# Second layer of the last two units as seven block products of 96 tokens

## The chip, the cores and the metric

The kernel runs on one core of a Trainium2 chip. The metric is device time in microseconds (us) of one execution. Engines are called as in the profile: PE is TensorE (PEld its weight loads), DVE is VectorE, ACT is ScalarE, POOL is GpSimd, and SP issues the DMAs.

## What is computed

Attention with a pooled and a banded part gives `x` (4 batches of 576 tokens, 512 features). Then come a Fourier mixing of `x`, a normalisation, a two-layer network and a gated convolution layer:

```python
u = x + real(fft(fft(x, axis=1), axis=2))
un = (u - mean(u)) / sqrt(var(u) + 1e-6)
x = u + maximum(un @ w_ch1, 0) @ w_ch2          # 512 -> 2048 -> 512
gate = sigmoid(sum over k of conv_w[k] * x shifted by 4 - k tokens)
out = (gate * (x @ w_val)) @ w_out
```

The change concerns the product with `w_ch2` (the second layer).

## The kernel before

**Units.** The two-layer network and the gated layer run over 12 units of 192 tokens, numbered 0 to 11, three to a batch. Features lie on the partitions. Each float32 operand is split into two float16 numbers, high and low, and each product of two operands is three matmuls (`PASS`: high by high, high by low, low by high), each with its own weight load.

**First layer.** In units 6 to 11 (`SEVEN`) the first layer is done by `seven(i)`, i from 0 to 3: weights and activations are cut into two by two blocks, tokens into two halves of 96, and seven block products with sums of blocks take the place of eight. The tile `r1` collects the results (DVE adds, one ACT copy); its four rows are the blocks of h: r[0:2] the first half of the hidden features, r[2:4] the second, each for 2 by 96 tokens in two chunks. `relu` turns them into `hh` and `hl` (high on ACT, low on DVE). The sums of weights that these products need are made once on DVE (`sums_w1`), stored in DRAM as `sums` and loaded for each unit (`load_sums`): into a place among the weights for even i, and from unit `S_TWO` on into tiles `sm` in the pool qkv for odd i.

**Second layer.** `c_group(g)`, g from 0 to 7, multiplies two chunks of 128 hidden features with w_ch2: 2 chunks by 4 output blocks by 3 passes, 24 matmuls of 192 tokens. The eight groups of a unit make 192 matmuls, accumulated in two PSUM banks `pc` (pool ps_c). `fin` adds the banks to X with two DVE instructions.

**Gated layer.** `split_y` splits the new X into `yy` (high on ACT, low on DVE), `conv` and for unit 11 `conv_last` make the taps of the convolution (DVE; one block of unit 11 on PE, `tps`), `val` multiplies with w_val, the gated product is split into `gh` and `gl`, and `out_tile` multiplies with w_out, 12 matmuls of 512 columns to a tile of 128 tokens. Units 10 and 11 share three such tiles.

**Order.** A table `ORDER` fixes, engine by engine, the order of all instructions of the whole kernel after the load of the constants, SP's DMAs among them. Nothing is chosen at run time: an engine, and SP's queue too, waits at an instruction whose input is late, and all that stands behind it waits with it. `SLOT` says which buffer of a pool a tile takes.

Of the kernel before, what the change touches and what calls it, by code (L numbers as in the profile page):

```python
# [21 lines left out]
UT = 192  # L22
# [47 lines left out]
450.0 430.1 430.0 499.0 488.1 488.0 467 499.1 488.2 491.1 491.0 492.1 491.2 492.0 492.2 499.2-3 493.1 493.0 493.2  # L70
546.0-1 539 535 546.2-3 545.0 550.1 550.0 545.1 553 554 559.1 559.0 609 639
# [6 lines left out]
170.1-2 210 186 187 172.0 197.1 197.0 247.0 171.0 211 171.1-2 172.3 172.1 172.4 212 193.1 172.5 172.2 174.0-1 227  # L78
247.1-2 193.2 247.3 174.2 197.2-3 228 197.4 224.0-1 253.0 197.5 173 247.4 229 258 247.5-6 188 259 253.1 239.0 239.3
232 189 239.4 239.1 255.2 230 239.5 239.2 255.0-1 255.3 265 224.2-3 225 234 233 241 249.3 249.0 253.2 269 224.5 224.4  # L80
253.3-5 292.0 236 292.1 274 257.0 257.3 253.6-7 292.2 249.1 249.4 278 243 249.5 249.2 253.8-10 302.0 246 253.11 292.3
257.1-2 261.0 253.12 302.2 253.13 261.1 257.4-5 263.3 263.0 299.0 302.1 253.14 293.0 284 407.0 302.3 251 292.4-5 288
263.1-2 263.4 261.2 303.3 303.1 261.3 263.5 303.2 267.1 304.1 293.1 293.3 304.2-3 300 293.4 303.0 261.5 261.4 293.2
267.0 299.1 305 293.5 295 271.0 310 273.0 271.2 271.1 273.2 273.1 261.6 271.3 314 275.1 299.2 273.3 275.0 323 306.1
296.0 277.1 277.0 275.2 277.2 327 299.3-4 335 296.1 280.0 306.2 280.1 282.0 407.1 296.2 407.2 296.3-4 283.0 304.0
296.5 282.1 283.1 306.3 297.0-1 306.0 309 407.4 285 297.3-5 286 291.0-1 338 291.2 342 297.2 291.3 294.0 291.4 322
326.1 326.0 294.1-2 350.1 313.0 326.2 291.5 339 291.6 326.3 313.1 333.1 333.0 298.0 311.0 354 350.0 298.2 298.1 357
311.1 364 407.3 328.3 328.1 328.0 328.2 329.1-2 329.0 331.2 331.1 329.3 332 334.2 334.1 371 331.3 331.0 334.0 334.3
341.0 319 341.1 379 347.0 324 344 347.1-2 345.0-1 355.0 333.2 356.0 333.3 347.3-4 388 355.2 359.0 462.1 366 355.1
347.5-6 356.2 359.2 347.7 345.2 355.3 356.1 345.3 356.3 347.8 395 376.0 376.3 347.9 400 359.3 359.1 378.0-2 347.10  # L90
361.1 378.3 361.0 406.1 361.3 406.0 378.4 376.1-2 376.4 361.2 413 381.0 372.0 376.5 372.1 410 377.0 387.0 381.3 377.1
# [393 lines left out]
def attn_moe_kernel(ctx, tc, q_t, k_t, v_p, v_w, w1, w2, w_val, conv_t, w_out, c_feat, c_seq, c_band, c_eye, c_plm, out):  # L485
# [44 lines left out]
    def load(**kw):  # L530
        nc.sync.dma_start(**kw)
# [1591 lines left out]
```

## Time and profile before

| | us |
|---|---|
| median of 3 runs | 657.6 |
| lowest and highest run | 655.76 and 657.8 |
| the profiled execution | 656.75 |
| its span, first to last instruction | 654.7 |
| PE busy, share of the span | 644.5, 98% |
| DVE busy | 527.3, 81% |
| ACT busy | 355.3, 54% |
| POOL busy | 103.5, 16% |

A time of the profile is counted from the start of the span; the execution's own time is some 2 us longer than the span. "Idle before" is the time that an engine stood still before an instruction, with what ended it. Matmuls are pipelined: the time from one start to the next is what a matmul costs in a stream, not its own length.

### The profile page before, as it was taken

To read this page: it belongs to the slowest core of one execution; us is meant where nothing else is said; L and a number is where in the kernel's file an instruction comes from. 1 tells how busy PE (TensorE), PEld (TensorE's weight loads), DVE (VectorE), ACT (ScalarE), POOL (GpSimd) and SP (SyncE) were. 2 spreads that over 40 slices of the span, in tenths; PEclk is the share of its full clock that TensorE was granted. 3 is DMA by queue.
4 is the path that set the end of the run, shared out by engine and by line. 5 is a ranking of instruction groups with operands and counts; after the bars stand their busy time and mean duration, and the time that the engine had idled before them with its cause. 6 is when DMAs were issued, how large, how long until landed. Compare 5 with 4: busy or idle time off the path is not lost.

```text
span 654.7 us, 20391 instructions
## 1 busy us (share of the span) xinstructions
PE 644.5 (98%) x8626; PEld 574.5 (88%) x8627; DVE 527.3 (81%) x1138; ACT 355.3 (54%) x1057; POOL 103.5 (16%) x162
## 2 busy tenths in 40 slices
PE   9989999999999999999999999999999999999997
PEld 4668899999998887998988888997899989998995
DVE  3999989989988876789999969996778787587554
ACT  2787659788644656677444778644232332414223
POOL 0000121310121703510310153032010100100000
PEclk9959999999999999999999999999999999999999
DMA  9994583023343012332482363352524234343201
GB/s 313 393 339 165 210 309 117 20 85 138 108 126 129 2 37 69 102 115 90 137 288 82 116 215 117 112 177 77 180 85 163 98 112 133 113 146 130 99 3 48
DMA packets 44301, 89.96 MB, mean 137 GB/s; under 512 B 3391, under 2 KB 24895, under 8 KB 43186
## 3 DMA queue, kind: packets, MB, share of 16 engines
q1 hardware_dynamic: 44210, 88.67, 39.8%
q8 instruction: 67, 1.10, 0.7%
q14 instruction: 24, 0.20, 0.1%
HBM read 73.77 MB, written 16.65 MB: 138 GB/s over the span
## 4 chain that ended last, share of the span: by engine, by line
PE 85%; DVE 7%; DMA 3%; ACT 2%; POOL 1%; issue 1%; SPq 0%; ACTq 0%; DVEq 0%; POOLq 0%
PE pc L1389 25%; PE ph L1319 11%; PE ph L1340 8%; PE out L1510 7%; PE val L1494 6%; PE p L1340 6%; DVE W L522 3%; PE ab L1070 2%; PE pc L1294 1%; PE po L1761 1%; PE dO L879 1%; PE po L1604 1%; DMA raw<-in_moe_w_ch_dram 1%; PE st L1154 1%; PE sc L957 1%; PE po L1002 1%
## 5 line engine op out<-in xcount | busy, mean ns | idle before, releaser
L1389 PE MATMUL pc<-hh,W 128*128 128x192 f16 x1232 | 169.8, 246 | 0.0
L1389 PEld LDWEIGHTS <-W 128*128 128x128 f16 x1848 | 152.7, 98 | 4.0 <-issue 1.6
L1389 PE MATMUL pc<-hl,W 128*128 128x192 f16 x616 | 129.3, 246 | 0.0
L1319 PE MATMUL ph<-u,W 128*128 128x192 f16 x960 | 94.5, 246 | 0.6 <-ACT u L1199 0.6
L1319 PEld LDWEIGHTS <-W 128*128 128x128 f16 x960 | 80.2, 98 | 2.8 <-issue 1.4
L1340 PEld LDWEIGHTS <-W 128*128 128x128 f16 x1632 | 79.0, 98 | 2.7 <-issue 0.8
L522 DVE SCALAR_TENSOR_TENSOR W<-X,cw,W 128x192 f32<-128x192 f32 x160 | 62.5, 426 | 9.1 <-ACT W L1457 8.8
L1340 PE MATMUL ph<-u,W 128*128 128x96 f16 x960 | 65.1, 206 | 0.2
L1352 ACT ACTIVATE hh<-r 128x384 f16<-128x384 f32 x48 | 24.3, 519 | 71.9 <-DVE r L528 60.2
L1494 PE MATMUL val<-yy,W 128*128 128x192 f16 x576 | 59.1, 246 | 0.1
L1494 PEld LDWEIGHTS <-W 128*128 128x128 f16 x576 | 47.6, 98 | 2.0 <-issue 0.9
L1340 PE MATMUL p<-u,W 128*128 128x96 f16 x672 | 47.9, 206 | 0.0
L1510 PE MATMUL out<-W,gh 128*128 128x512 f16 x144 | 45.8, 379 | 0.0
L528 DVE TENSOR_TENSOR r<-ph,r 128x384 f32<-128x384 f32 (+1 forms) x48 | 21.8, 454 | 21.0 <-PE ph L1340 19.2
L843 ACT ACTIVATE dP<-dS,dmx 128x64 f32<-128x64 f32 x120 | 36.5, 331 | 0.4
L522 DVE SCALAR_TENSOR_TENSOR hl<-r,hh 128x384 f16<-128x384 f32 x48 | 26.2, 564 | 9.4 <-ACT hh L1352 8.9
L528 DVE TENSOR_TENSOR r<-p,r 128x192 f32<-128x192 f32 (+1 forms) x72 | 28.2, 419 | 5.5 <-PE p L1340 3.1
L1323 ACT ACTIVATE hh<-ph 128x384 f16<-128x384 f32 x40 | 19.4, 490 | 19.5 <-PE ph L1319 17.6
L522 DVE SCALAR_TENSOR_TENSOR W<-W,W 128x1024 int32<-128x1024 int32 x24 | 28.9, 1220 | 0.2
L1510 PE MATMUL out<-W,gl 128*128 128x512 f16 x72 | 27.3, 379 | 0.0
L843 ACT ACTIVATION_READ_ACCUMULATOR dP<-dS,dmx 128x1 f32 x120 | 26.9, 224 | 0.0
L1510 PEld LDWEIGHTS <-gh 128*128 128x128 f16 x144 | 14.1, 98 | 13.6
(308 smaller groups left out, 1429.5 us busy)
## 6 DMA issues: line engine op xcount, KB each, us to landing
W<-sums SPq DMA_DIRECT2D x32, 512.0 KB, 4.4
W<-in_moe_w_ch_dram SPq DMA_DIRECT2D x12, 1024.0 KB, 6.9
sm<-sums SPq DMA_DIRECT2D x16, 512.0 KB, 6.7
out_dram<-osb SPq DMA_DIRECT2D x17, 256.0 KB, 4.1
vw<-in_vw_dram SPq DMA_DIRECT2D x8, 512.0 KB, 4.8
w1f<-W SPq DMA_DIRECT2D x8, 512.0 KB, 3.1
sums<-so SPq DMA_DIRECT2D x16, 256.0 KB, 2.9
v<-in_vp_dram SPq DMA_DIRECT2D x24, 144.0 KB
```

Source lines behind the costliest of these rows:

```text
L522: return eng.scalar_tensor_tensor(out=out, in0=in0, scalar=scalar, in1=in1, op0=op0, op1=op1)
L528: return eng.tensor_tensor(out=out, in0=a, in1=b, op=ALU.add)
L843: A.activation(out=s_[:, z, a], in_=pss[par][:, z, a], func=AF.Exp, scale=SCALE, bias=mx[:, par, z, a:a + 1], accum_out=su[:, par, z, a:a ...
L879: T.matmul(out=pos[x][par * 64:par * 64 + 64, a2, o:o + nq], lhsT=vw[g][row, 2 * z + hf, c:c + D], rhs=pts[z][row, par, a2, hf * 64:hf * 6 ...
L1070: T.matmul(out=ps[0:n, c0:c1], lhsT=d[x][:, c, sd, e, n0:n0 + n], rhs=feat[:, w, c, c0:c1], start=(t == 0), stop=(t == 5),)
L1319: T.matmul(out=ps[:, e], lhsT=w1_ap(pw, kc, 2 * g + e), rhs=uh[px][:, kc, :], start=(t == 0), stop=(t == 11))
L1323: A.activation(out=h_, in_=ps, func=AF.Relu)
L1340: T.matmul(out=out[:, e * HT:e * HT + HT], lhsT=w(pw, kc, e), rhs=b_[x](px, kc), start=(kc, pw, px) == (0, 0, 0), stop=(kc, pw, px) == (1, ...
L1352: A.activation(out=h[0], in_=x, func=AF.Relu)
L1389: T.matmul(out=ps[m // 2][:, m % 2], lhsT=w2_ap(pw, kk, m), rhs=x[px][:, e], start=(kk == 0 and (pw, px) == (0, 0) and m % 2 == 0), stop=( ...
L1494: T.matmul(out=ps[:, e], lhsT=wv_ap(pw, kc, 2 * mh + e), rhs=m_["y"][px][:, kc, :], start=(t == 0), stop=(t == 11))
L1510: T.matmul(out=ps, lhsT=(gh, gl)[px][:, kc, t * 128:(t + 1) * 128], rhs=wo_ap(pw, kc), start=(n == 0), stop=(n == 11))
```

## The change

In units 10 and 11 (`BOTH`) the second layer is cut in the same way as the first. `c_seven(i)` makes seven products, each of 2 output blocks by 2 chunks by 3 passes, 12 matmuls of 96 tokens: 84 for an i, 336 for a unit in place of 192 matmuls of 192 tokens. They are accumulated in three PSUM banks, 14 areas; the third bank is taken from the pool ps_t, so the third tile of `seven` moves from there to ps_h. Three things are added for it:

- Sums of blocks of h. `seven` now writes relu back to `r1` on ACT, POOL makes four sums of 192 columns (`r2`), and these are split into `hs` (high on ACT, low on DVE, 768 columns). `hh`/`hl` of the first half are made for one of the two token halves alone.
- Sums of blocks of w_ch2. The eight float32 weight tiles are stored to DRAM (`store_w2`, 8 DMAs of 512 KB) before they are split; later `sums_w2` loads them (16 DMAs of 256 KB), scales them on ACT, makes four differences of 256 columns on POOL, splits them (high on ACT, low on POOL, 1024 columns), and stores `sums2` (16 DMAs of 256 KB), eight times over. `load_sums2` loads them for units 10 and 11 (24 DMAs, 4 MB a unit).
- `fin_seven` in place of `fin`: one ACT, eight DVE and four POOL instructions.

`S_TWO` goes from 8 to 9: unit 8 loads all its sums of w_ch1 into the one place among the weights. The tables ORDER and SLOT are new from about the middle of the kernel on; before it, only the eight stores are put into SP's order.

```diff
-S_TWO = 8
+S_TWO = 9
+BOTH = (10, 11,)
+S_F32B, S_SUMSB = 0.4, (8.0, 9.4)
...
+    def store_w2(i):
+        nc.sync.dma_start(out=w2f[i * P:(i + 1) * P, :], in_=W[AT[8 + i] + 1])
+
+    def sums_w2(i, e):
...
+        A.activation(out=x, in_=x, func=AF.Copy, scale=sc["s2"][:, 0:1])
+        for o, p, q in ((0, 1, 0), (1, 3, 1), (3, 3, 0), (2, 2, 3)):
+            G.tensor_tensor(out=x[:, o], in0=x[:, p], in1=x[:, q], op=ALU.subtract)
+        y = [mainp["S"].tile([P, 4, 256], F16, tag="S", name="to") for _ in range(2)]
+        A.activation(out=y[0], in_=x, func=AF.Copy)
+        G.tensor_tensor(out=y[1], in0=x, in1=y[0], op=ALU.subtract)
...
-            x = pst("p5", [P, 2, UT])
+            x = ps_x["t"].tile([P, 2, UT], F32, tag="t", name="p5", slot=0) if two else pst("p5", [P, 2, UT])
...
-            relu(hy, r[:, 2:4])
-            p = pst("p5", [P, UT])
+            if two:
+                A.activation(out=r[:, 2:4], in_=r[:, 2:4], func=AF.Relu)
+                A.activation(out=hy[0], in_=r[:, 2:4], func=AF.Copy)
+                V.tensor_tensor(out=hy[1], in0=r[:, 2:4], in1=hy[0], op=ALU.subtract)
+            else:
+                relu(hy, r[:, 2:4])
+            p = ps_h.tile([P, UT], F32, tag="h", name="ph") if two else pst("p5", [P, UT])
...
+            A.activation(out=r[:, 0:2], in_=r[:, 0:2], func=AF.Relu)
+            A.activation(out=hx[0][:, 0], in_=z[0], func=AF.Copy)
+            V.tensor_tensor(out=hx[1][:, 0], in0=z[0], in1=hx[0][:, 0], op=ALU.subtract)
+            y = accp.tile([P, 4, UT], F32, tag="acc", name="r2", slot=1)
+            add(G, y[:, 0], z[1], z[3])
+            for o, p, q in ((y[:, 1], y[:, 0], z[0]), (y[:, 2], z[0], z[1]), (y[:, 3], z[2], y[:, 1])):
+                G.tensor_tensor(out=o, in0=p, in1=q, op=ALU.subtract)
...
+            A.activation(out=w[:, 0], in_=y, func=AF.Copy)
+            V.tensor_tensor(out=w[:, 1], in0=y, in1=w[:, 0], op=ALU.subtract)
...
+            todo = [(1, blk(0, 0), lambda px: hx[px][:, 0]), (2, blk(1, 0), lambda px: hy[px][:, 0]),
+                    (4, sm2(2), lambda px: hy[px][:, 1]), (6, sm2(3), ws(1)), (3, blk(1, 1), ws(3)),
+                    (7, sm2(1), ws(2)), (5, sm2(0), ws(0))]
+            if i == 3:
+                todo = [todo[k] for k in (0, 3, 4, 5, 6, 1, 2)]
...
+            A.activation(out=t[:, 0], in_=ps[1], func=AF.Copy, scale=iv)
+            add(G, x11, x11, t[:, 0])
+            more(t[:, 1], ps[6], t[:, 0])
+            more(t[:, 2], ps[5], t[:, 1])
+            more(t[:, 1], ps[7], t[:, 1])
+            add(G, x12_, x12_, t[:, 2])
+            add(G, x21, x21, t[:, 1])
+            add(G, x22, x22, t[:, 1])
+            for m in range(2):
+                more(x12_[:, m], c["ps"][3][m], x12_[:, m])
+            more(x22, ps[5], x22)
+            more(x11, ps[2], x11)
+            more(x21, ps[4], x21)
...
+    for i in range(8):
+        put(S_F32B, lambda i=i: store_w2(i))
+    spread([(1.0, lambda i=i, e=e: sums_w2(i, e)) for i in range(4) for e in range(2)], *S_SUMSB)
```

Three places of the new order. First DVE at the end of unit 11, from its last `r1` to the split of X; `pc` are the PSUM banks of the second layer, `t` is the tile of `fin_seven`. Before:

```order
L528 TENSOR_TENSOR r_10959<-p_11017,r_10959 128x384
L522 SCALAR_TENSOR_TENSOR hl<-r_10959,hh 128x384 x2
L522 SCALAR_TENSOR_TENSOR gl<-W_123,gh 128x2x192
L522 SCALAR_TENSOR_TENSOR X<-pc_10571,iv_1484,X 128x2x192
L522 SCALAR_TENSOR_TENSOR X<-pc_10572,iv_1484,X 128x2x192
L522 SCALAR_TENSOR_TENSOR tap<-X,cw,tap 128x192 x4
L522 SCALAR_TENSOR_TENSOR yy<-X,s_y_9697,yy 128x768
```

Now, from the split of the sums of h on:

```order
L1451 TENSOR_TENSOR hs<-r_11506,hs 128x768
L1432 TENSOR_TENSOR hl<-r_11401,hh 128x384
L542 SCALAR_TENSOR_TENSOR W_123<-W_123,val 128x384
L542 SCALAR_TENSOR_TENSOR gl<-W_123,gh 128x2x192 x2
L542 SCALAR_TENSOR_TENSOR t_11682<-pc_11083,iv_1494,t_11682 128x192
L542 SCALAR_TENSOR_TENSOR t_11682<-pc_11084,iv_1494,t_11682 128x192 x2
L542 SCALAR_TENSOR_TENSOR X<-pc_11085,iv_1494,X 128x2x96
L542 SCALAR_TENSOR_TENSOR X<-pc_11083,iv_1494,X 128x96
L542 SCALAR_TENSOR_TENSOR X<-pc_11084,iv_1494,X 128x96
L542 SCALAR_TENSOR_TENSOR X<-pc_11084,iv_1494,X 128x2x96
L542 SCALAR_TENSOR_TENSOR X<-pc_11085,iv_1494,X 128x2x96
L542 SCALAR_TENSOR_TENSOR tap<-X,cw,tap 128x192 x2
```

Two instructions that read PSUM stood between the last matmul of the second layer and the taps; now there are eight, and two taps instead of four stand ahead of the split `yy`.

The second place is PE right behind, from the last of 12 `out` matmuls of another tile to the product with w_val. Before:

```order
L1510 LDWEIGHTS gh
L1510 MATMUL out<-W_122,gh 128x512
L1467 MATMUL tps<-X,W_123 128x192 x5
L1494 LDWEIGHTS W_121
L1494 MATMUL val<-yy,W_121 128x192
```

Now:

```order
L1648 MATMUL out<-W_122,gh 128x512
L1605 MATMUL tps<-X,W_123 128x192 x2
L1632 LDWEIGHTS W_121
L1632 MATMUL val<-yy,W_121 128x192
L1632 LDWEIGHTS W_121
L1632 MATMUL val<-yy,W_121 128x192
L1605 MATMUL tps<-X,W_123 128x192 x2
```

The five taps that PE makes are spread out: two, then two matmuls of `val`, then two, and the last one later among `val`.

The third place is POOL while batch 3 is mixed; `vr`, `ptv`, `fs` and `uc` belong to attention, mixing and normalisation, `tx` and `to` to `sums_w2`. Before:

```order
L528 TENSOR_TENSOR vr<-vr,ptv 72x256
L528 TENSOR_TENSOR uc<-X 128x384
L528 TENSOR_TENSOR uc<-uc 128x192
L1044 TENSOR_TENSOR fs<-X 128x577 x2
L528 TENSOR_TENSOR sq<-sq 128x384
```

Now:

```order
L548 TENSOR_TENSOR vr<-vr,ptv 72x256
L1293 TENSOR_TENSOR tx<-tx 128x256 x6
L1064 TENSOR_TENSOR fs<-X 128x577
L548 TENSOR_TENSOR uc<-X 128x384
L1293 TENSOR_TENSOR tx<-tx 128x256
L1064 TENSOR_TENSOR fs<-X 128x577
L548 TENSOR_TENSOR uc<-uc 128x192
L548 TENSOR_TENSOR sq<-sq 128x384
L548 TENSOR_TENSOR sq<-sq 128x192
L1293 TENSOR_TENSOR tx<-tx 128x256
L1296 TENSOR_TENSOR to<-tx,to 128x1024
```

The differences of the weights stand between POOL's work for mixing and normalisation, and the long `to` behind them.

## Rows read from the trace of the kernel before

**Rows 1.** The page's first part: busy time, share of the span and instructions.

```profile
PE 644.5 (98%) x8626; PEld 574.5 (88%) x8627; DVE 527.3 (81%) x1138; ACT 355.3 (54%) x1057; POOL 103.5 (16%) x162
```

**Rows 2.** Windows: length; busy PE, PEld, DVE, ACT, POOL; granted clock; DMA share, GB/s.

```profile
455.00:635.00 180.00, 179.96 (x2779) 169.50 (x2777) 131.65 (x310) 55.63 (x112) 10.12 (x12) 1.00 0.34 115
```

**Rows 3.** Waits of PE from 50 us on, longest first in total.

```profile
PE dO L879 <- DMA vw<-in_vw_dram: 0.9, 1, 0.9
```

**Rows 4.** PE in order of time: start, length, line, operation, count.

```profile
600.88 1.14 PE L1340 MATMUL p<-u,W 128*128 128x96 f16 x23
...
641.77 4.12 PE L1494 MATMUL val<-yy,W 128*128 128x192 f16 x48
```

**Rows 5.** DVE groups by form, 300 to 655 us: busy us, mean ns, idle before.

```profile
L522 DVE SCALAR_TENSOR_TENSOR W<-X,cw,W 128x192 f32<-128x192 f32 x115 | 45.0, 425 | 6.7 <-ACT W L1457 6.5
L522 DVE SCALAR_TENSOR_TENSOR hl<-r,hh 128x384 f16<-128x384 f32 x48 | 26.2, 564 | 9.4 <-ACT hh L1352 8.9
L528 DVE TENSOR_TENSOR r<-p,r 128x192 f32<-128x192 f32 x48 | 17.0, 355 | 5.5 <-PE p L1340 3.1 <-PE st L1154 0.5
...
L528 DVE TENSOR_TENSOR r<-p,r 128x384 f32<-128x384 f32 x24 | 13.2, 549 | 0.0
...
L522 DVE SCALAR_TENSOR_TENSOR X<-pc,iv,X 128x384 f32<-128x384 f32 x16 | 9.4, 606 | 6.0 <-PE pc L1389 6.0
...
L1200 DVE TENSOR_TENSOR u<-uc,u 128x768 f16<-128x768 f32 x7 | 6.7, 953 | 0.2 <-ACT u L1199 0.2
```

**Rows 6.** ACT groups by form, 300 to 655 us.

```profile
L1352 ACT ACTIVATE hh<-r 128x384 f16<-128x384 f32 x48 | 24.3, 519 | 71.9 <-DVE r L528 60.2 <-PE pc L1389 11.4
...
L1252 ACT ACTIVATE so<-sx,s_w 128x1024 f16<-128x1024 f32 x6 | 6.9, 1144 | 8.7 <-DVE sx L1250 7.5 <-DMA sums<-so 1.3
...
L1199 ACT ACTIVATE u<-uc 128x768 f16<-128x768 f32 x7 | 5.9, 842 | 9.1 <-PE ph L1340 5.7 <-DVE uc L1209 2.9 <-DVE uc L525 0.5
```

**Rows 7.** POOL groups by form, whole span.

```profile
L528 POOL TENSOR_TENSOR vr<-vr,ptv 72x256 f32<-72x256 f32 x12 | 10.4, 873 | 0.6
...
L525 POOL TENSOR_TENSOR dP<-dP,dsu 128x512 f32<-128x512 f32 x8 | 8.3, 1057 | 16.1 <-DVE dsu L847 13.7 <-ACT dmx L838 2.4
...
L528 POOL TENSOR_TENSOR uc<-uc 128x192 f32<-128x192 f32 x6 | 4.8, 794 | 0.3
...
L525 POOL TENSOR_TENSOR r<-r 128x192 f32<-128x192 f32 x4 | 2.0, 507 | 0.3
```

**Rows 8.** DVE and then POOL in order of time, 428 to 436 us.

```profile
428.26 0.82 DVE L522 SCALAR_TENSOR_TENSOR FL<-fF,s_x,FH 128x578 f16<-128x578 f32 x1
...
432.08 1.97 DVE L522 SCALAR_TENSOR_TENSOR FL<-fF,s_x,FH 128x578 f16<-128x578 f32 x1
...
431.70 3.63 POOL L1044 TENSOR_TENSOR fs<-X 128x577 f32<-128x577 f32 x2
```

**Rows 9.** All engines in order of time, around the end of unit 11's second layer.

```profile
637.68 0.25 PE L1389 MATMUL pc<-hh,W 128*128 128x192 f16 x1
...
637.97 0.62 DVE L522 SCALAR_TENSOR_TENSOR X<-pc,iv,X 128x384 f32<-128x384 f32 x1 [0.21 <-PE pc L1389]
...
638.98 0.92 ACT L1436 ACTIVATE yy<-X,s_y 128x768 f16<-128x768 f32 x1
...
639.94 1.01 DVE L522 SCALAR_TENSOR_TENSOR yy<-X,s_y,yy 128x768 f16<-128x768 f32 x1
...
645.73 0.38 PE L1510 MATMUL out<-W,gh 128*128 128x512 f16 x1
```

**Rows 10.** DMA issues by line: count, KB each, median us from issue to landing.

```profile
W<-sums SPq DMA_DIRECT2D x32, 512.0 KB, 4.4
...
w1f<-W SPq DMA_DIRECT2D x8, 512.0 KB, 3.1
```

**Rows 11.** SP and ACT in order of time, 125 to 133 us.

```profile
125.10 0.30 SPq L531 DMA_DIRECT2D v<-in_vp_dram  x1
...
132.04 1.15 ACT L689 ACTIVATE W<-W,s_w 128x1024 f16<-128x1024 f32 x1
```

More of the change, by code (lines that the diff above doesn't have):

```diff
@@ L82 @@
[L82 to L91, printed above, removed]
@@ L1328, in mlp_steps @@
         sm = {}
+        two = b * UPB + j in BOTH
         def seven(i):
@@ new lines, in seven, with acc2 @@
+            hh[i] = (hx, hy, w)
+        def acc2():
+            if "ps" not in c:
+                b0, b1 = (ps_c.tile([P, 5, HT], F32, tag=f"c{z}", name=f"pc{z}") for z in range(2))
+                b2 = ps_x["t"].tile([P, 4, HT], F32, tag="t", name="pc2", slot=1)
+                c["ps"] = {1: (b0[:, 0], b0[:, 1]), 6: (b0[:, 2], b0[:, 3]), 3: (b0[:, 4], b1[:, 4]),
+                           7: (b1[:, 0], b1[:, 1]), 5: (b1[:, 2], b1[:, 3]), 2: (b2[:, 0], b2[:, 1]), 4: (b2[:, 2], b2[:, 3])}
+                c["pair"] = {1: b0[:, 0:2], 6: b0[:, 2:4], 7: b1[:, 0:2], 5: b1[:, 2:4], 2: b2[:, 0:2], 4: b2[:, 2:4]}
+            return c["ps"]
@@ new lines, in c_seven @@
+        def c_seven(i):
+            ps = acc2()
+            hx, hy, w = hh.pop(i)
+            t_ = c.pop(("sum", i))
+            bank = lambda n, m: (m if n == 3 else {1: 0, 6: 0, 7: 1, 5: 1, 2: 2, 4: 2}[n])
+            blk = lambda dk, dm: lambda p, e, m: w2_ap(p, 8 * dk + 2 * i + e, 2 * dm + m)
+            sm2 = lambda s: lambda p, e, m: t_[s][:, e * 512 + p * 256 + m * 128:e * 512 + p * 256 + m * 128 + 128]
+            ws = lambda s: lambda px: w[:, px, s]
+            todo = [(1, blk(0, 0), lambda px: hx[px][:, 0]), (2, blk(1, 0), lambda px: hy[px][:, 0]),
[3 more added lines that the diff above has]
+                todo = [todo[k] for k in (0, 3, 4, 5, 6, 1, 2)]
+            seq_ = [(n, m, f, x, e, pw, px) for n, f, x in todo for m in range(2) for e in range(2) for pw, px in PASS]
+            b_ = [bank(n, m) for n, m, *_ in seq_]
+            for k, (n, m, f, x, e, pw, px) in enumerate(seq_):
+                T.matmul(out=ps[n][m], lhsT=f(pw, e, m), rhs=x(px)[:, e * HT:e * HT + HT],
+                         start=(i == 0 and b_[k] not in b_[:k]), stop=(i == 3 and b_[k] not in b_[k + 1:]))
@@ new lines, in fin_seven @@
+        def fin_seven():
+            X, iv, ps = st[b]["X"], sc["iv12"][:, 0:1], c["pair"]
+            o = PAD + j * UT
+            x11, x12_, x21, x22 = (X[:, 2 * z:2 * z + 2, o + n * HT:o + n * HT + HT] for n in range(2) for z in range(2))
+            t = prp.tile([P, 3, 2, HT], F32, tag="E", name="t2", bufs=3)
+            more = lambda o, p, q: stt(V, o, p, iv, q, ALU.mult, ALU.add)
+            A.activation(out=t[:, 0], in_=ps[1], func=AF.Copy, scale=iv)
[11 more added lines that the diff above has]
+            more(x21, ps[4], x21)
@@ L1403, in both, with both2 @@
                 sm[i] = [load_sums(b * UPB + j, i, q) for q in range(2)]
+            def both2(i):
+                c["sum", i] = load_sums2(i)
+            if two:
+                for i in range(4):
+                    steps.append(lambda i=i: (both(i), both2(i)))
+                    steps.append(lambda i=i: seven(i))
+                    if i:
+                        steps.append(lambda i=i: c_seven(i - 1))
+                steps.append(lambda: c_seven(3))
+                steps.append(fin_seven)
+                return steps
             done = []
```

593 lines of the change are left out of this document (324 added, 269 removed), and 4 rows, old and new, of the table ORDER.

## The prediction

> **What bounds the kernel now.** I read the page's first part, the windows, PE's waits, and then the timeline of PE. PE is busy 98% of the span [rows 1], and in the stretch in which units 8 to 11 run, 455 to 635 us, it is busy 179.96 of 180 us at full granted clock, 2.4 GHz [rows 2]. From 50 us on its longest wait is 0.9 us for one DMA [rows 3]. So what PE is given to do sets the time, and the reader should see that DVE (131.65 of 180 us), ACT (55.63) and POOL (10.12) have room in that stretch [rows 2]. The exception is the end: behind the last matmul of unit 11's second layer a chain through DVE and ACT leads to the last products, and there PE is covered only by what work is left over [rows 9].
>
> A busy PE says nothing of the price of one matmul, so I take that from starts in a stream. 23 matmuls of 96 tokens, each with its own weight load, take 1.14 us; a lone one is listed at 0.21 us, so (1.14 - 0.21)/22 = 0.042 us each; shorter and mixed streams give up to 0.0431, and I use 0.0428. 48 matmuls of 192 tokens take 4.12 us, a lone one 0.25: (4.12 - 0.25)/47 = 0.0824 us [rows 4].
>
> **What PE is saved.** Two units lose 192 matmuls of 192 tokens and get 336 of 96: 384 x 0.0824 = 31.6 us against 672 x 0.0428 = 28.8 us, so -2.9 us (-2.7 to -3.4 with 0.0431 and 0.042). The sum hangs on a small matmul costing half of a large one, though each has a weight load. The Trainium skill ("TensorE: Matmul & The Clock Gate", Back-to-back issue gap) speaks against that: it gives some 81 ns for a matmul in a real stream of loads and matmuls at 128 columns. By it, 672 x 0.081 = 54.4 us, and the change would lose some 23 us, an estimate from that page. The trace does not agree: its streams are such pairs, and 96 columns cost 0.043 us [rows 4].
>
> **What the other engines get.** All of this lies beside PE unless something is late.
>
> DVE: for each i the split of 384 columns becomes one of 192 (0.564 to 0.355), and 768 columns of `hs` (0.953) come in: +0.74 us, eight times 5.9; `fin_seven` has six instructions of 192 columns at 0.355 and two of 96 at under that where `fin` has two of 0.606, +1.5 us a unit [rows 5]. Together +9 us, hidden by DVE's 48 idle us of the stretch [rows 2].
>
> ACT: for each i two relus back into `r1` (0.519 each) and 768 columns (0.842), less for the halved copy, some +1.7 us, eight times 14; `sums_w2` sixteen times 1024 columns at 1.144, 18 us [rows 6]. 32 us more, beside 124 idle us [rows 2].
>
> POOL: 32 sums and 8 adds of 192 columns at 0.507 to 0.794, 20 to 32 us; 32 differences of 256 columns at up to 0.873, 28 us; eight splits of 1024, each twice the 1.057 of 512 columns, 17 us [rows 7]: some 65 to 77 us, most of it in the last 230 us, where POOL does little.
>
> DMA: the eight stores of w_ch2 come into SP's queue early. Three of them wait for weights that DVE has just made and stand ahead of loads of further weights that wait for the same DVE work, so those shift by the 0.4 us of an issue. The others stand behind loads for attention. The narrowest is that of the first w_ch2 tile, fourth behind a load issued at 125.10: by some 127 it is issued, and 3.1 us later, as w1f, landed [rows 10, 11]; its place is overwritten by an ACT instruction at 132.04 [rows 11]. So 0, and if it were later, all of ACT's queue behind it would move. Unit 8 loses its second place for sums. By my count of the order's matmuls between the last use of one and the first use of the next, 5.6 to 6.3 us are left for a load of 4.4 [rows 10] and two issues of 0.4: 0, with some 1 us to lose if two land together. The 24 new loads have over 13 us each between the last use of a buffer and the next.
>
> **The waits that it adds.** (1) The chain of the last i of unit 11. Behind the last first-layer matmul: two DVE adds (0.355, 0.549), a relu (0.52), four POOL sums one after the other (2.0 to 3.2), ACT's 0.84 and DVE's 0.95 [rows 5 to 7], with the hand-overs 5.4 to 6.6 us until the low half is there. PE's order has 90 matmuls of 96 and 26 of 192 to do meanwhile: 3.85 + 2.14 = 6.0 us. So 0 to 0.6 us of wait, I take 0.2. For the other seven i the order leaves 7 to 10 us.
>
> (2) The end. Let T be the start of the last second-layer matmul. Before, T is 637.68; X was complete at T + 0.9, the low half of `yy` at T + 3.3, and the first of the last 24 `out` began at 645.73, T + 8.05 [rows 9], with PE never waiting long. Now the product that `fin_seven` reads first ends 22 matmuls ahead of T, so DVE starts at T - 0.75 and needs six times 0.36 and two times 0.28: T + 2.0. Two of its last instructions also wait for three POOL adds that follow its first: T - 0.4 + 3 x (0.51 to 0.79) and then two DVE instructions, T + 1.8 to 2.7. I take X at T + 2.4. Then ACT's 0.92 and DVE's 1.01 [rows 9]: the low half at T + 4.5. PE has 12 `out` at 0.215, four taps at 0.36 and two `val` until T + 4.2, so it loses 0.3. DVE then has six of the eight taps of the first two blocks still to do (0.39 each): T + 6.9; tanh, the gated product and the high half, three instructions of some 0.55 with one tap between them, T + 9.0. The last `out` begin at T + 9.0 instead of 8.05: +1.0 us, with 0.3 to 1.7 as its bounds. I take 1.1 with what the split order of the taps may cost.
>
> (3) DVE beside POOL. A DVE instruction with its operands in SBUF takes much longer while POOL works: FL takes 0.82 alone and 1.97 under POOL's `fs` [rows 8], while adds from PSUM keep their length. POOL's new 70 us fall on a DVE that is 73% busy [rows 2]. If half of the 80 new instructions hold one of DVE's up for half their length, that is some 18 us of DVE; nearly all of it goes into DVE's 39 remaining idle us. I take 0.4 us for PE, with 0 and 4 as bounds.
>
> **Sum.** -2.9 + 0.2 + 1.1 + 0.4 = -1.2 us. The profiled execution of 656.75 would become 655.55. It lies 0.85 under the median, so for the median, 657.6, I say **656.4 us**. A change under 0.3%, some 2 us, can't be told from none.
>
> **Rivals.**
> - Faster: the end costs as little as its lower bound, the chains are covered, and the 0.9 us wait for `vw` [rows 3], whose load now stands earlier in SP's queue, goes too: -2.9 + 0.3 - 0.9 = -3.5, 654.1 us. For it: PE is full and the order gives every other chain 1 to 4 us of slack. Against it: eight instructions stand where two stood, on the one chain that PE waits for.
> - Slower: DVE, held up by POOL, falls behind in units 8 to 11. The three tiles of ps_h for each i now share two buffers, so a late add on DVE stops PE's next product at once; that decides if DVE's loss passes its 39 idle us, or if the loss comes in lumps of a 2 us `to` more than its slack of about 2 us. Eight `to` and eight chains with 0.3 to 0.5 us each that reach PE: +4 us, so -2.9 + 1.3 + 4 = +2.4, 660.0 us. For it: FL's 1.15 us of delay [rows 8]. The Trainium skill ("SBUF — State Buffer", Who interferes with whom) has the rule: a DVE instruction with two SBUF inputs and a GpSimd instruction that reads SBUF shut each other out for the whole instruction. The trace agrees: FL ends about when the first `fs` does.
> - It does not do what it says: a small matmul costs as much as a large one, +23 us, 680 us. Nothing in the rows bears it out.
>
> **How the numbers follow.** Forecast, within 0.3% of before: 0.45, its own range 655.6 to 658.5. Faster rival 0.32, slower 0.22, no saving 0.01. So faster 0.32, same 0.45, slower 0.23. The range reaches to the faster rival and to the slower one's time, 653.9 to 660.2, and leaves out those 2 in 10 that lie past either.
>
> **What would show it.** PE: 672 matmuls of L1479 at 0.043 us; if they come at 0.08 the first term is wrong. End: X complete 2.0 to 2.9 us behind the last second-layer matmul, and the last `out` 9 us behind it. PE waits naming `hs` or `hl` in the last i; waits of PE for DVE's `r` adds in units 8 to 11, and DVE instructions of 0.36 listed at 0.8 and more, would speak for the slower rival. A wait for `W<-sums` or `sm` would mean that unit 8's single place or SP's queue is too tight. The forecast is wrong if the waits of PE from 300 us to the end of unit 11 come to over 2 us, or if the end costs nothing.

## The result: 1% slower, and the profile after

| | before | after |
|---|---|---|
| median of 4 runs, us | 657.55 | 663.71 |
| lowest and highest run | 655.76 and 657.8 | 662.62 and 664.69 |
| the profiled execution, its span | 656.75, 654.7 | 664.69, 662.9 |

The ratio is 1.0098, 95% interval 1.0082 to 1.0115: 6.4 us slower by the ratio (the medians differ by 6.2), outside the range of the prediction. All line numbers below are those of the kernel spoken of; an edit that adds lines shifts them.

The first part of the page of after, against [rows 1]: PE is as busy as before, though it has less to do.

```profile
PE 644.9 (97%) x8914; PEld 573.3 (86%) x8915; DVE 547.6 (83%) x1158; ACT 383.4 (58%) x1099; POOL 174.7 (26%) x242
```

Windows of after (length; busy PE, PEld, DVE, ACT, POOL; granted clock; DMA share, GB/s). In the stretch of [rows 2] PE now stands still for 2.0 us, and DVE is 82% busy. The second and third line are the place where the granted clock fell: full until 407 us, behind two waits of PE, then 0.66 on the mean of 5 us, which is time at the lower level, 1.2 GHz. (1 - 0.66) x 5 = 1.7 us are lost there beside the waits themselves.

```profile
455.00:635.00 180.00, 178.00 (x2949) 164.42 (x2948) 146.93 (x324) 77.93 (x145) 68.30 (x82) 1.00 0.63 202
...
398.00:407.00 9.00, 7.37 (x90) 5.42 (x88) 7.86 (x19) 5.85 (x22) 5.80 (x6) 1.00 0.75 247
407.00:412.00 5.00, 5.00 (x67) 5.00 (x67) 2.52 (x11) 3.19 (x12) 0.00 (x0) 0.66 0.11 25
```

Waits of PE in after from 80 us on (total, times, longest). Before, the longest was 0.9 us for vw [rows 3]; the waits for ET, h, DS, r, dP and tm are new.

```profile
PE dO L899 <- DMA vw<-in_vw_dram: 1.6, 1, 1.6
PE po L1022 <- ACT ET L1017: 1.3, 1, 1.3
PE ph L1341 <- ACT h L1343: 1.2, 1, 1.2
PE p L1400 <- DVE DS L542: 0.8, 1, 0.8
PE ph L1400 <- DVE r L548: 0.8, 2, 0.6
PE dPT L882 <- DVE dP L545: 0.7, 1, 0.7
PE ph L1377 <- ACT u L1219: 0.6, 1, 0.6
PE pc L1479 <- DMA tm<-sums: 0.6, 1, 0.6
```

The end of unit 11 in after, all engines in order of time, against [rows 4, 9]. The 20 small matmuls take (1.01 - 0.21)/19 = 0.042 us each, as was reckoned. T is 644.79; X is complete at 646.89 (T + 2.1), the low half of `yy` at T + 4.1, and the last `out` begin at T + 8.5, where it was T + 8.05.

```profile
643.05 1.01 PE L1479 MATMUL pc<-hs,tm 128*128 128x96 f16 x20
...
644.79 0.21 PE L1479 MATMUL pc<-hh,tm 128*128 128x96 f16 x1
...
645.11 1.78 DVE L542 SCALAR_TENSOR_TENSOR X<-pc,iv,X 128x192 f32<-128x192 f32 x5
...
647.88 1.02 DVE L542 SCALAR_TENSOR_TENSOR yy<-X,s_y,yy 128x768 f16<-128x768 f32 x1 [0.16 <-ACT yy L1574]
...
653.29 0.60 PE L1648 MATMUL out<-W,gh 128*128 128x512 f16 x2
```

So the loss is neither in the new matmuls nor mainly at the end. It comes in three places: 90 to 165 us, where PE does exactly what it did before and the only new thing is the eight stores; 386 to 411 us; and the waits for DVE in units 7 to 11. Each has a theory of its own, tested below: theory 1, the stores hold up the loads behind them; theory 3, two loads stand at a bad place in SP's queue; theory 2, POOL's sums hold DVE up.

### The profile page after: what moved, and what is told of

Read it like the earlier page. It is cut to its first block, busy times and chain, and to the rows that moved or that the text cites. A ratio compares the mean times of both kernels' runs of the same rounds, so it can differ in the third digit from the quotient of the medians.

```text
span 662.9 us, 21279 instructions
## 1 busy us (share of the span) xinstructions
PE 644.9 (97%) x8914; PEld 573.3 (86%) x8915; DVE 547.6 (83%) x1158; ACT 383.4 (58%) x1099; POOL 174.7 (26%) x242
## 4 chain that ended last, share of the span: by engine, by line
PE 77%; DVE 10%; DMA 8%; POOL 2%; ACT 2%; issue 1%; SPq 0%; DVEq 0%; POOLq 0%; ACTq 0%
PE pc L1515 18%; PE ph L1377 11%; PE ph L1400 7%; PE val L1632 6%; PE out L1648 6%; PE p L1400 5%; PE pc L1479 4%; DVE W L542 4%; PE ab L1090 2%; PE pc L1352 1%; DMA tm<-sums 1%; DMA raw<-in_moe_w_ch_dram 1%; PE po L1899 1%; DMA vw<-in_vw_dram 1%; PE po L1022 1%; PE po L1742 1%
## 5 line engine op out<-in xcount | busy, mean ns | idle before, releaser
L1515 PE MATMUL pc<-hh,W 128*128 128x192 f16 x1008 | 138.4, 246 | 0.0
L1515 PEld LDWEIGHTS <-W 128*128 128x128 f16 x1512 | 125.0, 98 | 4.6 <-issue 1.8
L1515 PE MATMUL pc<-hl,W 128*128 128x192 f16 x504 | 104.5, 246 | 0.0
L1400 PEld LDWEIGHTS <-W 128*128 128x128 f16 x1728 | 84.7, 99 | 4.5 <-issue 1.5
L1377 PEld LDWEIGHTS <-W 128*128 128x128 f16 x960 | 80.2, 98 | 3.6 <-issue 2.0
L1400 PE MATMUL ph<-u,W 128*128 128x96 f16 x1056 | 69.2, 207 | 1.0 <-DVE r L548 0.8
L542 DVE SCALAR_TENSOR_TENSOR W<-X,cw,W 128x192 f32<-128x192 f32 x160 | 66.0, 453 | 2.6 <-ACT W L1595 2.3
L1400 PE MATMUL p<-u,W 128*128 128x96 f16 x672 | 51.6, 209 | 0.8 <-DVE DS L542 0.8
L1632 PEld LDWEIGHTS <-W 128*128 128x128 f16 x576 | 47.5, 98 | 2.8 <-issue 1.3
L548 DVE TENSOR_TENSOR r<-ph,r 128x192 f32<-128x192 f32 (+1 forms) x56 | 24.5, 438 | 18.7 <-PE ph L1400 17.3
L1293 POOL TENSOR_TENSOR tx<-tx 128x256 f32<-128x256 f32 x32 | 26.4, 828 | 48.1 <-ACT tx L1291 26.9
L1412 ACT ACTIVATE hh<-r 128x384 f16<-128x384 f32 x32 | 15.8, 519 | 29.5 <-DVE r L548 27.2
L542 DVE SCALAR_TENSOR_TENSOR hl<-ph,hh 128x384 f16<-128x384 f32 x40 | 21.9, 551 | 5.9 <-ACT hh L1381 5.7
```

The costliest lines, as they stand in the source:

```text
L542: return eng.scalar_tensor_tensor(out=out, in0=in0, scalar=scalar, in1=in1, op0=op0, op1=op1)
L548: return eng.tensor_tensor(out=out, in0=a, in1=b, op=ALU.add)
L1293: G.tensor_tensor(out=x[:, o], in0=x[:, p], in1=x[:, q], op=ALU.subtract)
L1377: T.matmul(out=ps[:, e], lhsT=w1_ap(pw, kc, 2 * g + e), rhs=uh[px][:, kc, :], start=(t == 0), stop=(t == 11))
L1400: T.matmul(out=out[:, e * HT:e * HT + HT], lhsT=w(pw, kc, e), rhs=b_[x](px, kc), start=(kc, pw, px) == (0, 0, 0), stop=(kc, pw, px) == (1, ...
L1412: A.activation(out=h[0], in_=x, func=AF.Relu)
```

## Experiments

Medians in us and ratios to the kernel before, which ran beside them on the same chip each time (its median 656.96 to 657.53):

| kernel | median | ratio, 95% interval |
|---|---|---|
| e1 before + stores | 661.74 | 1.0062 (1.0039 to 1.0086) |
| e2 stores on ACT's queue | 660.67 | 1.0048 (1.0030 to 1.0066) |
| e3 little work for POOL | 661.39 | 1.0059 (1.0038 to 1.0080) |
| e4 two loads moved | 662.09 | 1.0068 (1.0042 to 1.0093) |
| e5 = e2 and e4 | 657.48 | 1.0010 (0.9994 to 1.0025) |
| e6 = e5, sums moved | 658.47 | 1.0010 (0.9997 to 1.0023) |
| e7 = e6, last tiles exchanged | 658.07 | 1.0006 (0.9993 to 1.0019) |
| e8 = e7, ACT's sums further back | 660.83 | 1.0050 (1.0031 to 1.0069) |
| e9 = e5, little work for POOL | 655.98 | 0.9967 (0.9949 to 0.9986) |
| e10 = e5, sums at other places | 659.16 | 1.0022 (1.0006 to 1.0038) |
| e11 three stores behind the loads | 662.81 | 1.0080 (1.0051 to 1.0108) |
| e12 the changed kernel again | 664.69 | 1.0116 (1.0094 to 1.0138) |

Gains below are differences of ratios from the first 1.0098 of the changed kernel, where nothing else is said. Its second ratio, 1.0116 in e12, shows that a difference of 0.2% between two chips says little by itself.

**The stores: e1, e2, e11, e12.** e1 adds to the kernel before what the first half of the change adds, and no more:

```diff
+    w2f = dram.tile([8 * P, 1024], F32, tag="w2f", name="w2f")
+    def store_w2(i):
+        nc.sync.dma_start(out=w2f[i * P:(i + 1) * P, :], in_=W[AT[8 + i] + 1])
```

> The kernel before, with nothing added but the eight stores of w_ch2 (nobody reads them), at the same places of SP's queue as in the changed kernel. Theory 1 (the stores hold up the weight loads behind them, and PE with them, at 105 to 165 us): 2.0 to 2.5 us slower than before, about 659.9 us, and the same new waits of PE as in the changed kernel (about 1.2 us for h near 105 us, 0.7 us for dP near 118 us). Rival (those waits come from something else, or from chance): 657.5 us, and PE's first half as before.

Slower by 0.62%, 4.1 us, more than expected. Its two longest waits of PE, and the windows around the first: here the clock fell behind it, (1 - 0.72) x 6 = 1.7 us.

```profile
PE ph L1297 <- ACT h L1299: 2.1, 1, 2.1
PE dO L889 <- DMA vw<-in_vw_dram: 1.8, 1, 1.8
```

```profile
100.00:106.00 6.00, 4.07 (x26) 3.77 (x24) 5.50 (x8) 6.00 (x25) 0.00 (x0) 1.00 0.27 94
106.00:112.00 6.00, 5.80 (x25) 5.80 (x26) 5.16 (x7) 5.03 (x20) 0.00 (x0) 0.72 0.81 263
```

e2 has the changed kernel issue the same stores from ACT, behind the instruction that reads the tile anyway:

```diff
-        nc.sync.dma_start(out=w2f[i * P:(i + 1) * P, :], in_=W[AT[8 + i] + 1])
+        nc.scalar.dma_start(out=w2f[i * P:(i + 1) * P, :], in_=W[AT[8 + i] + 1])
```

> The changed kernel, with the eight stores issued by ACT, each right behind the sum of squares that reads the same tile, instead of by SP; the rest of SP's queue stays in its order. Theory 1: 1.5 to 2.5 us faster than the changed kernel, 661.2 to 662.2 us; the waits of 1.2 and 0.7 us near 105 and 118 us go. Rival (it is the bytes of the stores on the DMA engines, not SP's queue, or ACT's issues cost as much): 663.7 us.

It gained 0.50%, 3.3 us, and its interval lies wholly under that of the changed kernel; the waits for h and dP are gone, 0.2 us is left of them. Its wait for vw is 0.3 us where it was 1.6, so not all of the gain lies between 90 and 165 us. But e2 moves the stores in time as well as to another queue, so it doesn't tell why they hurt. The trace of after does. SP issues the two loads into `raw` (weights as they come, which DVE then converts) at 87.52, no later than before (87.75 there). Yet DVE, whose rows follow in order of time, waits 3.68 us for the first (2.34 before). The same wait is 4.62 us in e1, 4.43 in e12 and 2.70 in e2.

```profile
96.91 0.43 DVE L641 TENSOR_SCALAR W<-raw 128x512 int32<-128x512 int32 x1 [3.68 <-DMA raw<-in_moe_w_ch_dram]
...
108.84 0.69 DVE L641 TENSOR_SCALAR W<-W 128x1024 int32<-128x1024 int32 x1 [0.59 <-DMA W<-in_moe_w_ch_dram]
```

e11 tests that. It moves three stores within SP's queue:

```diff
-L1283 DMA w2f<-W_118 128x1024
 L551 DMA W_123<-in_moe_w_ch_dram 128x2x1024
 L1262 DMA w1f<-W_114 128x1024
-L1283 DMA w2f<-W_119 128x1024
 L551 DMA raw<-in_moe_w_ch_dram 128x1024 x2
 L1262 DMA w1f<-W_117 128x1024
 L551 DMA W_122<-in_moe_w_ch_dram 128x2x1024
+L1283 DMA w2f<-W_118 128x1024
+L1283 DMA w2f<-W_119 128x1024
-L1283 DMA w2f<-W_120 128x1024
 L551 DMA W_123<-in_moe_w_ch_dram 128x2x1024
+L1283 DMA w2f<-W_120 128x1024
```

> The changed kernel with three of the eight stores moved in SP's queue, nothing else: the first two from ahead of the two raw loads of 87 us to behind them and the next two entries, the third from ahead of the load of weights at 103 us to behind it. Theory 1, as the traces have it now (SP issues the raw loads on time, but the 1 MB of stores issued just ahead of them shares the DMA engines, so the loads land late and DVE, ACT and PE wait): the wait of 1.2 us near 105 us and that of 0.7 near 118 us fall under 0.3 us together, and the kernel gains about what the stores on ACT's queue gained, 2 to 3.3 us: 660.1 to 661.4 us. Rival (SP's waits at the stores for DVE and ACT hold up what is behind them): the five stores that stay keep most of the loss, gain under 1 us.

> The changed kernel once more, beside the run above on the same chip, to see how much its waits and its time differ from one profile and one chip to another. All theories: 662.5 to 664.5 us, 0.8 to 1.15% above the kernel before, with the waits near 105 and 118 us. If its time fell under 661.5 us here, the gains of the other runs would be that much smaller.

e11 against e12: 1.0080 to 1.0116, 2.4 us. The two intervals overlap a little, and against the first 1.0098 it is 1.2 us, so the time alone doesn't prove the gain; the trace shows what changed. SP in e11 issues the raw loads at 88.07 and the stores at 90.89, and DVE's wait is 1.49 us; no wait of PE near 105 or 118 us is left.

```profile
88.07 0.88 SPq L553 DMA_DIRECT2D raw<-in_moe_w_ch_dram  x2
...
90.89 1.66 SPq L1285 DMA_DIRECT2D w2f<-W  x2
```

```profile
95.64 0.43 DVE L643 TENSOR_SCALAR W<-raw 128x512 int32<-128x512 int32 x1 [1.49 <-DMA raw<-in_moe_w_ch_dram]
```

So it is the stores ahead of the loads. The 1 MB ahead of the raw loads does not make their issue late; it makes them land late. The third store stands ahead of a load of weights and would fit the wait at 118 us, but e11 moves all three together and can't part them. The Trainium skill has this in "DMA: Bandwidth & Descriptors" (Queues, rings and completion order): each DMA engine takes the descriptors of one queue in their order. The trace agrees: behind the stores the first raw load is used 9.4 us after its issue (96.91 - 87.52), ahead of them 7.6 us (95.64 - 88.07).

e12 also shows how far one kernel's profiles differ: its wait for h is 1.9 us where the first profile had 1.2, and its clock fell at 107 and at 387 us instead of at 407, the second time behind 1.8 us for vw.

**The loads in the middle: e4, e5.** Around 400 us in after, all engines in order of time. A 256 KB load of `tx` and a 512 KB load of sums are issued just ahead of a 144 KB load `v`. POOL waits 1.42 us for that `v`, ACT for POOL, and PE for ACT.

```profile
396.63 0.35 SPq L551 DMA_DIRECT2D tx<-w2f  x1
...
397.08 0.38 SPq L551 DMA_DIRECT2D W<-sums  x1
...
397.55 0.35 SPq L551 DMA_DIRECT2D v<-in_vp_dram  x1
...
402.76 0.73 POOL L548 TENSOR_TENSOR vr<-v 72x256 f32<-72x256 f32 x1 [1.42 <-DMA v<-in_vp_dram]
...
405.41 0.41 ACT L1017 ACTIVATE ET<-eT 72x288 f32<-72x288 f32 x1 [2.32 <-POOL vr L548]
...
405.87 1.18 PE L1022 MATMUL po<-ET,vr 72*64 72x144 f32 x8 [1.26 <-ACT ET L1017]
```

```diff
-L551 DMA vw<-in_vw_dram 128x1024
 L551 DMA v_6223<-in_vp_dram 72x2x256
+L551 DMA vw<-in_vw_dram 128x1024
...
+L551 DMA v_6240<-in_vp_dram 72x2x256
 L551 DMA tx<-w2f 128x512
 L551 DMA W_116<-sums 128x1024
-L551 DMA v_6240<-in_vp_dram 72x2x256
```

> The changed kernel with two loads moved in SP's queue: the second vw behind the next v instead of ahead of it, and the last v of the window values ahead of a 256 KB load of w2f and a 512 KB load of sums instead of behind them. Theory 3 (DMAs that stand together in the queue make the one that PE waits for late): the wait for vw falls from 1.6 to 0.9 us, the wait for ET at 406 us from 1.3 to under 0.3 us, and the clock stays up at 407 us: 2.5 to 3.7 us faster than the changed kernel, 660.0 to 661.2 us. Rival (POOL or DVE is late there anyway): the wait for ET stays, at most 0.7 us are gained, 663.0 us.

It gained 0.30%, 2.0 us, with an interval that overlaps that of the changed kernel; the wait for ET is gone and the clock stays up, as the window shows.

```profile
398.00:412.00 14.00, 13.50 (x192) 11.01 (x191) 11.61 (x35) 11.60 (x40) 6.45 (x9) 1.00 0.65 220
```

The wait for vw is 1.1 us here; over all profiles it ranges from 0.2 to 1.8 us, 1.8 in e1 too, where vw stands as before. In all seven kernels whose stores ACT issues it is 0.2 to 0.4 us; with the stores on SP's queue it is 0.4 in e3 and 1.0 to 1.8 in the others. The eight stores are issued 250 us earlier, so why they should matter there stays open.

> The changed kernel with both edits of the two runs before it: the eight stores issued by ACT, and the two loads moved in SP's queue. Theories 1 and 3 together (two separate losses): the gains add, 3.3 + 2.0 us by the ratios of those runs, so some 5 us faster than the changed kernel and 0 to 1.5 us slower than before, 657.5 to 659 us, with no drop of the clock between 50 us and the end. Rival (one loss, seen twice: the later waits only come from the shifted first half): no more than the better of the two alone, 660 us.

1.0010: the two gains add, 3.3 + 2.0 reckoned, 5.8 measured. From e2 to e5, which differ in the two loads alone, it is 2.5 us, and these intervals don't overlap. With its stores issued by ACT and two loads moved, the changed kernel can't be told from the kernel before.

**POOL: e3, e9, e6, e7, e8, e10.** What is left of the loss is DVE. In after, DVE and POOL in order of time: POOL's `to` of 2.2 us falls on DVE's taps, which take 3.93/6 = 0.66 us each where they had 0.425 [rows 5]; DS, behind them, is 0.8 us late for PE. To test theory 2, e3 leaves out nearly all of POOL's work on the sums: each difference is taken over 8 of 256 columns, and each low half is filled with zeros.

```profile
457.32 3.93 DVE L542 SCALAR_TENSOR_TENSOR W<-X,cw,W 128x192 f32<-128x192 f32 x6
...
457.48 2.23 POOL L1296 TENSOR_TENSOR to<-tx,to 128x1024 f16<-128x1024 f32 x1
...
461.44 0.93 DVE L542 SCALAR_TENSOR_TENSOR DS<-pp,ivx,qs 128x289 f32<-128x289 f32 x2
```

```diff
-            G.tensor_tensor(out=x[:, o], in0=x[:, p], in1=x[:, q], op=ALU.subtract)
+            G.tensor_tensor(out=x[:, o, 0:8], in0=x[:, p, 0:8], in1=x[:, q, 0:8], op=ALU.subtract)
-        G.tensor_tensor(out=y[1], in0=x, in1=y[0], op=ALU.subtract)
+        G.memset(y[1].bitcast(F32), 0.0)
```

> The changed kernel with little work for POOL in the sums of w_ch2: the 32 differences are taken over 8 columns of 256, and each of the eight low halves is a memset; all instructions, DMAs and bytes stay. Theory 2 (POOL's 45 us of sums make DVE and POOL's other work late): PE's new waits between 400 us and the end of unit 11 and the drop of the clock at 407 us go, together 4 to 6 us: 658 to 660 us. Rival (these waits come from the new orders and from the DMAs that stand in SP's queue): less than 1.5 us, 662.2 to 663.7 us, with the drop of the clock still there.

It gained 0.39%, 2.6 us, between the two expectations. The waits for r and DS went, but the one for ET and the fall of the clock stayed. So theory 2 holds for units 7 to 11 and not for 400 us. The same edit on e5:

> The kernel of e5 with little work for POOL in the sums of w_ch2, cut as in e3. Theory 2: what e5 still loses between 430 and 500 us (waits of 0.6 and 0.8 us and small ones) is DVE held up by POOL's sums; it goes, and the kernel is 1.5 to 2.5 us faster than e5, 655.5 us, which is what the saved matmuls leave. Rival: without POOL's work DVE and ACT are late there all the same, from the orders alone: less than 0.5 us faster than e5.

0.9967 against 1.0010: 2.8 us, and 0.33% faster than before. This is what the saved matmuls would leave if POOL's work on the sums were free. e9 does not part DVE's lengthened instructions from POOL's own other work, which also comes earlier there; the rows above show the first. Its waits of PE from 405 us on:

```profile
PE st L1181 <- ACT osb L1673: 1.4, 1, 1.4
PE ph L1407 <- ACT r L1424: 0.2, 1, 0.2
PE val L1639 <- DVE yy L549: 0.2, 1, 0.2
PE out L1655 <- DVE uc L1190: 0.2, 1, 0.2
```

The 1.4 us are an ACT scaling of the sums that waits for its load of w2f, ahead of the copy that frees PE's bank; they are there in e2, e4 and e12 too, with 0.9 to 1.7 us, and not in the first profile of after. Can the sums be placed so that they hold nobody up? Three tries. e6:

```diff
 POOL TENSOR_TENSOR uc<-X 128x384
-POOL TENSOR_TENSOR tx<-tx 128x256
 POOL TENSOR_TENSOR fs<-X 128x577
...
 POOL TENSOR_TENSOR sq<-sq 128x192
+POOL TENSOR_TENSOR tx<-tx 128x256
...
-POOL TENSOR_TENSOR to<-tx,to 128x1024
 POOL TENSOR_TENSOR X<-X,DS 128x287
+POOL TENSOR_TENSOR to<-tx,to 128x1024
...
-ACT ACTIVATE tx<-tx,s_w 128x1024
-ACT ACTIVATE to<-tx 128x1024
 ACT ACTIVATE r<-ph 128x192
 ACT ACTIVATE osb<-out,sof 128x512
+ACT ACTIVATE tx<-tx,s_w 128x1024
+ACT ACTIVATE to<-tx 128x1024
```

> The kernel of e5 with four more moves: on POOL one difference of the weights goes behind the squares of batch 3 and one low half behind the add of the mixed X, on ACT a scaling and a high half of the weights go behind the copy of an output tile. No work is taken away. Theory 2, narrowed (it is where the sums stand on POOL and ACT that makes DVE's r, DVE's DS and ACT's output copy late, at 443, 461 and 494 us): those three waits of PE, 0.6 + 0.8 + 1.1 us or more, shrink to under 0.5 us together, 1.5 to 2.5 us faster than e5. Rival (DVE has too much to do there wherever POOL's work stands, so the waits move along): less than 0.7 us faster than e5.

The rival was right: 1.0010 like e5. The wait for r at 437 us went, and 1.0 us for yy and 0.5 us for hh came at 492 and 495 us. e7 exchanges the last two output tiles in the orders of PE, ACT and SP:

> The kernel of e6 with the last two output tiles exchanged, so that the tile whose result is copied in two halves by ACT and DVE comes last, as in the kernel before. Theory 4 (the longer way from PE's last matmul to the end, 4.5 us against 4.0, is the copy of a whole tile by one engine): 0.4 to 0.6 us faster than e6. Rival (that way is set by the DMA alone): the same as e6.

The rival was right. The way from the start of PE's last matmul to the end of the span is 4.1 us in e6 and in e7, and the time, 1.0006, can't be told from e6. The 4.5 us of after are not due to the tile: e3 ends with the same tile and takes 4.0, e1 ends as the kernel before does and takes 4.4. e8 moves the two ACT instructions once more:

```diff
-ACT ACTIVATE tx<-tx,s_w 128x1024
-ACT ACTIVATE to<-tx 128x1024
 ACT ACTIVATE W<-X,cw 128x192
 ACT ACTIVATE yy<-X,s_y 128x768
 ACT ACTIVATE sq<-uc 128x768
+ACT ACTIVATE tx<-tx,s_w 128x1024
+ACT ACTIVATE to<-tx 128x1024
```

> The kernel of e7 with the two ACT instructions of the weight sums at 486 us put three places further back, behind the split of X and the squares of the next unit. In e6 and e7 they stood ahead of that split, and PE waited 1.0 us for yy and 0.5 us for what followed. Theory 2, narrowed: each instruction of the sums costs PE what it holds up behind it on an in-order engine, so both waits go and the kernel is 1.0 to 1.7 us faster than e7, 656.0 to 656.7 us, a little under the kernel before. Rival: the waits move to the next place, as they did from e5 to e6, and it is the same as e7 within 0.4 us.

Slower by 0.44% than e7, neither of the two. The POOL instructions that wait for those of ACT moved with them, onto DVE's adds of squares. DVE and POOL in e8, and PE behind them; then the same adds in e10, where POOL is idle:

```profile
493.12 3.17 DVE L563 TENSOR_TENSOR sq<-sq 128x384 f32<-128x384 f32 x2
...
492.95 2.12 POOL L1311 TENSOR_TENSOR to<-tx,to 128x1024 f16<-128x1024 f32 x1
495.03 1.84 POOL L1308 TENSOR_TENSOR tx<-tx 128x256 f32<-128x256 f32 x2
...
496.43 0.66 PE L1189 MATMUL st<-sq,ones 128*128 128x192 f32 x2 [2.72 <-DVE sq L563]
```

```profile
492.81 0.94 DVE L563 TENSOR_TENSOR sq<-sq 128x384 f32<-128x384 f32 x2
```

3.17 us against 0.94, and behind the wait of 2.72 us the clock fell as well. This is the rule of the Trainium skill that the prediction named ("SBUF — State Buffer", Who interferes with whom): a DVE instruction with two SBUF inputs and a GpSimd instruction that reads SBUF shut each other out for a whole instruction. The trace agrees: the first of the two adds, begun behind `to`, is listed at 2.37 us and ends at 495.49, 0.42 us behind the end of `to` at 495.07.

e10 goes back to e5, moves two POOL instructions as in e6 and the last tiles as in e7, and these two:

```diff
+POOL TENSOR_TENSOR to<-tx,to 128x1024
 POOL TENSOR_TENSOR tx<-tx 128x256 x2
-POOL TENSOR_TENSOR to<-tx,to 128x1024
...
-ACT ACTIVATE tx<-tx,s_w 128x1024
 ACT ACTIVATE to<-tx 128x1024
...
 ACT ACTIVATE W<-X,cw 128x192
+ACT ACTIVATE tx<-tx,s_w 128x1024
```

> The kernel of e5 with no work taken away, but POOL's and ACT's sums of w_ch2 at other places: on POOL one difference behind the squares of batch 3, one low half behind the add of the mixed X, another low half ahead of two differences; on ACT one scaling behind the taps at 495 us, so that neither it nor a low half on POOL falls on the split of X or on DVE's adds of squares; and the last two output tiles exchanged as in e7. Theory 2 (a long POOL instruction that falls on a DVE instruction which PE waits for is what the sums cost; e9 puts their whole cost at 2.8 us): 1.2 to 2.2 us faster than e5, 655.3 to 656.3 us, so below the kernel before by 0.2 to 0.35%. Rival (the sums can't be placed without meeting such an instruction: the waits move, as in e6 and e8): 657 us or more.

The rival again: 1.0022. DVE's next eight taps took the blow, 4.62/8 = 0.58 us each:

```profile
495.42 4.62 DVE L557 SCALAR_TENSOR_TENSOR W<-X,cw,W 128x192 f32<-128x192 f32 x8
```

```profile
PE p L1415 <- ACT DS L1155: 0.8, 1, 0.8
PE eT L1027 <- ACT yy L1589: 0.8, 1, 0.8
PE pc L1530 <- ACT hh L1427: 0.8, 1, 0.8
```

Of these waits of PE the first two stood in e5 too (0.8 for DS, 0.9 for yy). The third, for hh at 503 us behind those taps, is new; the one for r at 437 us is gone.

No kernel that does the whole work beat the kernel before; e5, e6 and e7 can't be told from it.

## Why the prediction was wrong, step by step

- **What PE is saved**, -2.9 us: right. 0.042 to 0.043 us for a matmul of 96 tokens in unit 11.
- **DMA**: this is the step that failed. The prediction put the eight stores at 0, because SP's queue moves by one issue only and each store lands before its place is overwritten. Both hold, and no wait for a store is listed. It did not ask what the stores' bytes do to the loads behind them. The raw loads, on which DVE, ACT and PE wait in turn, landed later: 3.3 us by e2, 4.1 us by e1 with one fall of the clock, and 2.4 us by e11 against e12 for three of the eight (1.2 against the first measurement).
- The same step speaks of the 24 new loads of sums for units 10 and 11, which did no harm but 0.6 us for `tm`, and not at all of the 16 loads of `tx` among attention's loads. The place of one of them and of a load of sums ahead of `v`, and the place of `vw`, cost 2.0 us by e4 and 2.5 us from e2 to e5, the fall of the clock behind them included.
- **(3) DVE beside POOL**, +0.4 with 0 and 4 as bounds: the mechanism was right, the size was off. 2.8 us by e9. The prediction let nearly all of DVE's delay vanish in its idle time; but idle time helps only what comes after it, since DVE works in the order of the table. The durations on POOL were right, as the groups of after show (busy us, mean ns, idle before): 0.83 us for a difference and 2.17 for a low half, where 0.87 and 2.1 were reckoned.

```profile
L1293 POOL TENSOR_TENSOR tx<-tx 128x256 f32<-128x256 f32 x32 | 26.4, 828 | 48.1 <-ACT tx L1291 26.9 <-DMA sm<-sums 11.2 <-DMA tx<-w2f 8.8
L1296 POOL TENSOR_TENSOR to<-tx,to 128x1024 f16<-128x1024 f32 x8 | 17.3, 2167 | 14.6 <-ACT W L1617 7.6 <-ACT to L1295 6.2 <-DMA sums<-to 0.8
```

- **(1) The last i of unit 11**, +0.2: no wait of PE for `hs` or `hl` there, 0.
- **(2) The end**, +1.1: 0.45 us at the start of the last `out`, T + 8.5 where T + 9.0 was foretold. X is complete at T + 2.1, foretold as T + 2.4. The 0.5 us more behind the last matmul in after's profile are not the change's: the kernels differ there by as much with either tile at the end.
- **The slower rival** (660.0 us, by DVE and POOL) named one of the three mechanisms, with a size of 4 us. That mechanism alone, as in e5, gives no slower kernel than before; it needed the other two. The faster rival let the wait for vw go; it grew from 0.9 to 1.6 us.
- **The sign of being wrong** came true: the waits of PE from 300 us to the end of unit 11 come to some 6 us, where over 2 us was to speak against the forecast.

The sum now: -2.9 + 3.3 for the stores + 2.0 for the loads at 400 us + 2.8 for POOL + 0.45 for the end = 5.65 us, where 6.4 was measured. With the 5.8 us that the two edits of e5 gain together in place of 3.3 + 2.0 it is 6.15 us. The rest was not traced further.

## What to carry to other kernels

A DMA added to a queue has two prices: the wait and issue on the queue, and the bytes that now travel ahead of the loads behind it. Look at what lands next behind it and who waits for that, even if each issue stays on time; here three of the stores could simply go behind the loads. And work given to GpSimd because it was idle was paid by VectorE here, where both worked on SBUF at the same time: before counting it as hidden, ask which VectorE instruction it will fall on and how soon TensorE needs that one.

## What was not expected of the hardware

- Behind a single wait of PE of 1.3 to 2.7 us, with PE nearly full before and behind it, the granted clock could fall from 2.4 to 1.2 GHz, at a price of 1.7 us: at 407 us in after, at 106 us in e1, at 497 us in e8 (behind 2.72 us), twice in e12. It did not each time: in e4 a wait of 1.9 us for h, and in e9 one of 1.4 us, left it at 1.00. So a wait of that length can cost 1.7 us on top of its own; what decides it, these runs don't show.
- Moving two ACT instructions three places back (e7 to e8) cost 2.9 us, 1.7 of them by the clock: POOL's instructions that depend on them moved onto two DVE adds.
